# The second layer's places in SBUF: unsplit operands take the longest free, ten w_out units in single tiles, the first input rows asked for ahead of w_in

## The chip, the cores and the metric

One core of one Trainium2 chip runs the whole program. The metric is device time in microseconds (us) of one launch; lower is better. The engines are TensorE (PE, with its weight loads as PEld), VectorE (DVE), ScalarE (ACT), GpSimd (POOL, unused here) and SyncE (SP), which issues nearly all transfers between HBM and SBUF.

## What is computed

Small attention between `x` and a state, in both directions, then two dense layers in float32:

```python
a = softmax(x @ state.T / 8);  xread = a @ state       # per batch and head
a2 = softmax(state @ x.T / 8); sread = a2 @ x
x = concat([xread, sread], axis=2)      # (8, 544, 512) after heads are joined: 4352 rows
h = x @ moe_w_in;  x = (s * relu(h) ** 2 + b) @ moe_w_out       # 512 -> 2048 -> 512
h = x @ moe2_w_in; out = (h / (1 + exp(-h))) @ moe2_w_out       # 512 -> 2048 -> 512
```

## The kernel before

Every product of float32 operands is made of three matmuls: an operand is split into a high part (ACT copies it to fp32r) and a low part (DVE subtracts), and high x high, high x low and low x high are summed in PSUM.

The first layer and the attention run over nine blocks of columns: the eight batches (512 rows each) and a last block `"s"` with the 256 state rows. Each block has 16 steps `f`: `mm1_a(f)` (L634), relu on ACT (L680), square on DVE (L681), `gh` on ACT (L686), `gl` on DVE (L687), and three steps later (`LAG`) `mm2_a(f)` (L701). `r` has three buffers; the block's result is pulled from PSUM into `op` and two `r` buffers, and `end_a` stores it to `x2` in HBM (L739). Block `"s"` runs with the split units of `w_in` themselves: `split_next` splits two units that `load32` (L171, four transfers of 32 rows for each of the two) has brought to a `mid` tile, and asks for the pair two further on.

The second layer is a Strassen-like scheme with seven products `A11 ... A22` instead of eight. Columns are cut into five pieces of 512, 512, 384, 384, 384. **First product** (`first_product`): for each piece, eight `Quad`s of seven steps; a step is one product of six matmuls (L1005), then the operations of `Quad.rest`: pulls of PSUM banks (ACT, L229), sums (DVE, L852), silu (ACT, L1038). `Quad.put` (L1041) writes seven combinations to `go` in HBM. In the middle of a piece `load_inputs` asks for the next piece's eight input tiles (L959), later DVE sums them and ACT and DVE split them. **Second product** (`Chunks`, `Sums`): `go` is read back (L1238), each chunk is split five to six steps ahead, multiplied by the split `w_out`, summed and put out.

All engines run their instructions in the order in which the program issues them; the order is written by hand (`hooks`, `extra`, `after(n, op)`, which runs `op` n steps later).

All of SBUF that the first layer no longer needs is handed to the second one in *places* of 128 x 512 words. `vacate(tag, n)` puts a whole tile of n places into the list `free`. `Place(dtype)` takes one: F32 for unsplit operands (inputs, raw weights, a quad's sums, chunks), F32R for split ones.

```python
of = [k for k, x in enumerate(free) if x[2] is dtype]      # parts of tiles cut for dtype
whole = [k for k, x in enumerate(free) if x[2] is None]    # tiles with all parts free
k = of[0] if of and len(whole) <= 8 else min(of[:1] + whole[:1])
```

A whole tile is cut for one type when its first part is taken; when all its parts have been given back it is whole again (`give`), and the next taker may cut it for the other type. A place is given back in program order, when the last instruction that uses it has been issued; the next taker's first instruction waits until that use has ended.

Of the kernel before, what the change touches and what calls it, by code (L numbers as in the profile page):

```python
# [3 lines left out]

# [1 line left out]

# [6 lines left out]
F32 = mybir.dt.float32  # L13
F32R = mybir.dt.float32r
# [6 lines left out]
B, H, S, NS, D = 8, 8, 512, 32, 64  # L21
DM, DFF = 512, 2048
P = 128
# [10 lines left out]

FIRST_PAIRS = "i0 i1, i2 i3, i4 i5, i6 i7, o0 o1, i8 i9, o2 o3, i10 i11, o4 o5, i12 i13, o6 o7, i14 i15, o8 o9, o10 o11, o12 o13, o14 o15"
PLAIN = (12, 13,)
FIRST = """
L.0.0 L.0.1 L.1.0 L.1.1 Lsbd.0 Lxt.0 A.0.0 Lsg.1 B.0.0.0 B.0.1.0 A.0.1 B.0.2.0 B.0.0.1 B.0.3.0
A.1.0 B.0.1.1 B.1.0.0 B.0.2.1 A.1.1 B.1.1.0 B.1.0.1 B.0.3.1 B.1.1.1 L.2 B.1.2.1 Lsg.2 B.1.2.0
# [25 lines left out]
AGAIN = (8, 9, 10, 11, 6, 7, 4, 5, 0, 1, 2, 3, 8, 9, 10, 11)  # L65
# [8 lines left out]
def fused_kernel(ctx: ExitStack, tc, xt, xn, sbd, sg, w1, w2, sv, bv, out):  # L74
# [29 lines left out]
    def space(tag, shape=(P, S), dtype=F32R):  # L104
        return wpool.tile(list(shape), dtype, tag=tag, name=tag)

    def pair(tag, dtype=F32):
        return space(tag, (P, 2, S), dtype)
# [19 lines left out]
    wh, wl, raw, w32 = {}, {}, {}, {}  # L128
# [16 lines left out]
    def new32(of):  # L145
        if starting and of[0][0] == "i":
            t = flat(rotated("early", "q10 q15 q14" + "".join(f" w{u}" for u in PLAIN)))
        elif starting and of[0][1] in PLAIN:
# [85 lines left out]
    ring = {}  # L234

    def hi_w(w, dve=False):
        t, i = w
        ring[w] = pair(f"w{i}" if t == "o" else f"q{AGAIN[i]}", F32R)
        wh[w] = ring[w][:, 0]
        copy(wh[w], w32[w], dve)  # L240

    def lo_w(w):
        t, i = w
        wl[w] = ring[w][:, 1]
        rest(wl[w], w32[w], wh[w])

    def split(hi, lo, x):
# [90 lines left out]
    two = {}  # L338
# [466 lines left out]
          for k, (_, n) in enumerate(pieces) for p in PRODUCTS}  # L805


    free, closing = deque(), []

    def vacate(tag, n=1):  # L810
        free.append((tag, n, None))

    class Place:
        def __init__(self, dtype=F32R):
            of = [k for k, x in enumerate(free) if x[2] is dtype]
            whole = [k for k, x in enumerate(free) if x[2] is None]
            k = of[0] if of and len(whole) <= 8 else min(of[:1] + whole[:1])
            tag, i, kind, *t = free[k]
            del free[k]
            if not t:  # L820
                two = space(tag, (P, i, S), dtype)
                free.extendleft((tag, n, dtype, two[:, n]) for n in range(i - 1, 0, -1))
                parts[tag], i, t = i, 0, [two[:, 0]]
            self.at, self.t = (tag, i, dtype, t[0]), t[0]

        def give(self):
            tag = self.at[0]
            if closing and tag.startswith("raw"):
                return
            free.append(self.at)  # L830
            whole = [k for k, x in enumerate(free) if x[0] == tag]
            if len(whole) == parts[tag]:
                for k in reversed(whole):
                    del free[k]
                vacate(tag, parts[tag])

    parts = {}

    clock, due = [0], {}

# [596 lines left out]
    def last_block(add):  # L1439

        def give(*tags):
            for tag in tags:
                add(f, 2, vacate, tag)

        splits = [(p, c) for p in RIGHT for c in range(2)]
        inputs[0] = Inputs(0)
        for f in range(NF):
            if f == 0:  # L1450
                give("sbd")
                for tag in ("xt", "xn", "xr0", "xr1", "q12", "q13", "q14"):
                    add(f, 2, vacate, tag, 2)
                for tag in ("xh1", "xl1"):
                    add(f, 2, vacate, tag, 2)
                for i in range(2):
                    add(f, 2, vacate, f"raw{i}", 4)
                add(f, 2, inputs[0].load)
            if f >= 2:
                add(f, 2, vacate, f"w{f - 2}", 2)  # L1460
            if f == 7:
                for tag in ("mid0", "mid1"):
                    add(f, 2, vacate, tag, 2)
                for i in range(4, 8):
                    add(f, 2, vacate, f"q{i}", 2)
            if f == 11:
                for i in range(4):
                    add(f, 2, vacate, f"q{i}", 2)
            if f == 15:
                for i in range(8, 12):  # L1470
                    add(f, 2, vacate, f"q{i}", 2)
            if 2 <= f < 4:
                for name in ("T1", "T2", "T3"):
                    add(f, 2, inputs[0].sum, name, f - 2)
            for i, what in ((f - 4, inputs[0].high), (f - 5, inputs[0].low)):
                if 0 <= i < len(splits) // 2:
                    for p, c in splits[2 * i:2 * i + 2]:
                        add(f, 2, what, p, c)
            for i, what in ((f - 6, "load"), (f - 9, "high"), (f - 10, "low")):
                if i >= 0 and i % 2 == 0 and i // 2 < 5:  # L1480
                    if what == "load":
                        quads[i // 2] = list(duos_in(i // 2))
                    for x in quads[i // 2]:
                        add(f, 2, getattr(x, what))
# [46 lines left out]
    def close():  # L1531

        closing.append(True)
        left = [x for x in free if not x[0].startswith("raw")]
        free.clear()
        free.extend(left)

    def extra(bi):
        k = order[bi]
        ops = {}  # L1540

        def add(f, when, op, *args):
            ops.setdefault((f, when), []).append(lambda: op(*args))

        if bi < B - 1:

            halves = [Half(k + 1, j) for j in range(2)]
            add(1 + (bi == 1), 2, score, k + 1, halves)
            add(1, 2, load_sbd, k + 2)
            add(2, 0, load_all, k + 2, xt)  # L1550
            names = "tr rd nb ex mx sb en n0 n1 n2 s0 s1 s2 s3 s4 tu pl ah al"
            when = (
                (1, 1, 1, 1, 3, 3, 3, 3, 3, 4, 6, 6, 6, 7, 7, 10, 11, 8, 8),
                (2, 2, 2, 2, 5, 5, 5, 5, 5, 8, 9, 9, 9, 10, 10, 10, 11, 11, 12),
            )
            for h, fs in zip(halves, when):
                for n, (f, name) in enumerate(zip(fs, names.split())):
                    add(f + (bi == 1 and n < 4), 2, getattr(h, name))
            add(12, 2, read, k + 1, halves)
            add(13, 0, load_all, k + 2, xn)  # L1560
            add(13, 2, pull_read, k + 1, halves)
        def add_g(f0, fs, *g):
            add(f0, 0, load_g, *g)
            for j in range(2):
                add(fs[j], 2, split_g, *g, j)

        if bi == 1:
            add_g(0, (1, 2), 1, 1)
            for n, u in enumerate(PLAIN):
                add(1 + n, 2, hi_w, ("o", u))  # L1570
                add(1 + n, 2, lo_w, ("o", u))
            one = softmax[1]
            add(0, 0, load_all, 1, xn)
            add(0, 0, load_sbd, 2)
            add(0, 0, load_all, 2, xt)
            for f, when, name, *args in (
                (0, 0, "n0"), (0, 0, "n1"), (0, 0, "n2", 0), (0, 0, "n2", 1), (0, 2, "tu", "a"),
                (0, 2, "pl"), (1, 2, "sr", "a"), (1, 2, "pu"),
            ):
                add(f, when, getattr(one, name), *args)  # L1580
            add(2, 0, load_all, 2, xn)
        if bi < B:

            for fg, (f0, *fs) in enumerate(((1, 4, 4), (3, 6, 7), (9, 12, 13), (11, 14, 15))):
                if fg < 2:
                    g = k, fg + 2
                elif k + 1 < B:
                    g = k + 1, fg - 2
                else:
                    continue  # L1590
                add_g(f0, fs, *g)
        for f in range(NF):
            for when in range(3):
                for op in later.pop((NF * bi + f, when), ()):
                    add(f, when, op)
        if bi == B - 1:
            for i, pair in enumerate(stream[:2]):
                add(5 + 3 * i, 0, load32, pair)
            for i in range(RING // 2):
                add(9 + 2 * i, 2, split_next)  # L1600
        if bi == B:
            for f in (0, 1, 4, 5):
                add(f, 2, split_next)
            last_block(add)
        return ops

    with tc.manual_schedule():
# [8 lines left out]
        act_places.appendleft("q15")  # L1616
        run(order, pend)
        for i in (NF - 2, NF - 1):
            vacate(f"w{i}", 2)
        for n in range(9):  # L1620
            vacate(f"{('r', 'gh', 'gl')[n // 3]}{n % 3}")
        for tag in ("wf0", "wf1", "xs", "q15", "xh0", "xl0", "op"):
            vacate(tag, 2)
        chunks = Chunks()
        to_load = iter([
            Duo(("O", i, p), ("O", i + 1, p)) for p in RIGHT for i in range(0, NF // 2, 2)
# [59 lines left out]
```

## Time and profile before

| | |
|---|---|
| median of 3 runs | 1344.69 us (1343.94 to 1345.14) |
| profiled execution | 1344.56 us, span of its instructions 1342.8 us |
| PE busy | 1303.1 us, 97% of the span |
| DVE, ACT busy | 979.5 us (73%), 705.3 us (53%) |
| mean granted TensorE clock | 0.994 of full speed |
| HBM traffic | 282.95 MB, mean 211 GB/s |

Block `"s"` lies at about 603 to 664 us, the first product follows, the second one ends at 1335, and the last results go out. Pieces 0 and 1 of the first product are at 664 to 739 and 739 to 814, pieces 2 to 4 at 814 to about 1000. Busy times count an instruction from its start to its end; matmuls overlap each other, so a busy PE says that no time without a matmul was seen, not that it is at its peak. A line number like L229 or L852 can be that of a helper (`copy`, `tt`) that many steps share.

### The profile page before, as it was taken

How to read it: one execution, taken by the hardware profiler on the slowest of the kernel's cores; microseconds unless marked ns; L12 is line 12 of the kernel's file. 1: busy time of each engine (PE TensorE's matmuls, PEld its weight loads, DVE VectorE, ACT ScalarE, POOL GpSimd, SP SyncE). 2: the span in 40 equal slices, each digit the busy share in tenths (PEclk: the TensorE clock that was granted, in tenths of full speed). 3: DMA queues.
4: the chain of work that ended last, by engine and by line, in shares of the span. 5: the costliest groups of instructions: out<-in, count | busy, mean ns of one | idle time of the engine just before them, and what ended most of it. 6: DMA issues, size and time to landing. Idle time of an engine off the chain costs nothing. (4 is left out here: it accounts for less than half of the span.)

```text
span 1342.8 us, 20818 instructions
## 1 busy us (share of the span) xinstructions
PE 1303.1 (97%) x7256; PEld 1102.7 (82%) x7256; DVE 979.5 (73%) x1745; ACT 705.3 (53%) x1273; POOL 0.7 (0%) x7
## 2 busy tenths in 40 slices
PE   5999999999999999999999999899999999999997
PEld 1555787888787878888988879899998888899997
DVE  7898798989897979756767647475767766665654
ACT  6885554545454545445655536364666634353542
POOL 0000000000000000000000000000000000000000
PEclk9999999999999999999999999999999999999999
DMA  9975664655555634515576465556699876777583
GB/s 340 323 270 217 224 227 157 205 179 204 189 181 173 206 146 142 195 48 160 156 265 245 184 212 205 199 187 209 219 316 353 286 219 208 209 228 233 167 268 77
DMA packets 171114, 282.95 MB, mean 211 GB/s; under 512 B 22272, under 2 KB 93952, under 8 KB 171008
## 3 DMA queue, kind: packets, MB, share of 16 engines
q1 hardware_dynamic: 170208, 281.22, 62.4%
q8 instruction: 57, 0.93, 0.3%
q10 hardware_dynamic: 800, 0.39, 0.1%
q14 instruction: 49, 0.40, 0.1%
HBM read 166.20 MB, written 115.34 MB: 210 GB/s over the span
## 5 line engine op out<-in xcount | busy, mean ns | idle before, releaser
L701 PE MATMUL bank<-gh,w 128*128 128x512 f32 (+1 forms) x880 | 278.6, 380 | 0.8 <-ACT q L229 0.8
L634 PE MATMUL bank<-xh,q 128*128 128x512 f32 (+1 forms) x624 | 202.8, 374 | 4.4 <-ACT r L680 3.2
L701 PEld LDWEIGHTS bank<-gh,w 128*128 128x128 f32 x880 | 163.8, 189 | 39.1 <-issue 5.9
L701 PE MATMUL bank<-gl,w 128*128 128x512 f32 (+1 forms) x440 | 166.7, 379 | 0.0
L634 PEld LDWEIGHTS bank<-xh,q 128*128 128x128 f32 x624 | 114.4, 189 | 35.9 <-issue 6.9
L681 DVE SCALAR_TENSOR_TENSOR r<-r,s_sb 128x512 f32<-128x512 f32 (+1 forms) x128 | 91.6, 715 | 47.6 <-ACT r L680 47.2
L680 ACT ACTIVATE r<-bank 128x512 f32<-128x512 f32 (+1 forms) x128 | 71.9, 562 | 91.0 <-PE bank L634 74.0
L634 PE MATMUL bank<-xl,q 128*128 128x512 f32 (+1 forms) x312 | 114.9, 368 | 0.0
L686 ACT ACTIVATE gh<-r,b_sb 128x512 fp32r<-128x512 f32 (+1 forms) x96 | 66.5, 693 | 58.5 <-DVE r L681 58.4
L1005 PE MATMUL bank<-q,w 128*128 128x384 f32 (+1 forms) x315 | 92.8, 357 | 3.9 <-DVE q L852 3.9
L701 PEld LDWEIGHTS bank<-gl,w 128*128 128x128 f32 x440 | 83.4, 190 | 15.0
L1005 PE MATMUL bank<-w,w 128*128 128x384 f32 (+1 forms) x319 | 88.0, 355 | 0.0
L701 PE MATMUL bank<-q,w 128*128 128x512 f32 (+1 forms) x384 | 87.5, 377 | 0.0
L1005 PE MATMUL bank<-w,q 128*128 128x384 f32 (+1 forms) x309 | 86.3, 358 | 0.0
L1005 PE MATMUL bank<-q,q 128*128 128x384 f32 (+1 forms) x283 | 81.9, 357 | 3.3 <-ACT q L229 3.3
L687 DVE SCALAR_TENSOR_TENSOR gl<-r,b_sb,gh 128x512 fp32r<-128x512 f32 (+1 forms) x96 | 68.5, 714 | 16.9 <-ACT gh L686 16.8
L701 PEld LDWEIGHTS bank<-q,w 128*128 128x128 f32 x384 | 69.0, 188 | 13.6 <-DVE op L727 0.5
L634 PEld LDWEIGHTS bank<-xl,q 128*128 128x128 f32 x312 | 59.1, 189 | 9.0 <-DVE mid L566 0.2
L1005 PEld LDWEIGHTS bank<-q,w 128*128 128x128 f32 x315 | 58.4, 189 | 9.5 <-DVE q L852 4.9
L229 ACT ACTIVATE q<-bank 128x384 f32<-128x384 f32 (+3 forms) x70 | 42.9, 613 | 39.5 <-PE bank L1005 20.6
L1005 PEld LDWEIGHTS bank<-w,w 128*128 128x128 f32 x319 | 58.6, 188 | 4.9
L1005 PEld LDWEIGHTS bank<-w,q 128*128 128x128 f32 x309 | 56.8, 188 | 5.2
(858 smaller groups left out, 2771.1 us busy)
## 6 DMA issues: line engine op xcount, KB each, us to landing
raw<-w SPq DMA_DIRECT2D x80, 512.0 KB, 5.1
go<-q SPq DMA_DIRECT2D x87, 192.0 KB, 2.0
q<-gd SPq DMA_DIRECT2D x27, 512.0 KB, 5.6
go<-q SPq DMA_DIRECT2D x51, 256.0 KB, 2.4
w<-go SPq DMA_DIRECT2D x68, 192.0 KB, 4.0
w<-go SPq DMA_DIRECT2D x40, 256.0 KB, 4.4
gd<-xr SPq DMA_DIRECT2D x18, 512.0 KB, 4.6
q<-go SPq DMA_DIRECT2D x36, 256.0 KB, 4.8
```

What stands on the lines that cost most here:

```text
L229: nc.scalar.activation(out=out, in_=x, func=AF.Copy)
L634: nc.tensor.matmul(ph[:, :n], a, x, start=j == 0 and i == 0, stop=j == last and i == 2)
L680: nc.scalar.activation(out=r, in_=ph[:, :n], func=AF.Relu)
L681: nc.vector.scalar_tensor_tensor(out=r, in0=r, scalar=s_sb, in1=r, op0=ALU.mult, op1=ALU.mult)
L686: nc.scalar.activation(out=gh, in_=r, func=AF.Identity, bias=b_sb)
L687: nc.vector.scalar_tensor_tensor(out=gl, in0=r, scalar=b_sb, in1=gh.bitcast(F32), op0=ALU.add, op1=ALU.subtract)
L701: nc.tensor.matmul(po[c][:, :n], a, x, start=f == 0 and i == 0, stop=f == NF - 1 and i == 2)
L1005: nc.tensor.matmul(bank[:, :n], a, x, start=start and j == 0 and i == 0, stop=stop and j == last and i == 2, skip_group_check=True,)
```

## The change

Places are now of two kinds. `carve` cuts a tile once, for good, into places of one type (`fixed[F32]` or `fixed[F32R]`). `vacate` hands over tiles of a single place, which either type may take (`spare`). Each place gets a stamp when it is given back. An F32R place comes from `fixed[F32R]` if that isn't empty, otherwise it is the longest free single tile. An F32 place is the longest free of `fixed[F32]` and `spare` together. To have enough single tiles, the split `w_out` units 0 to 9 get two single tiles each, `wh{i}` and `wl{i}`, where each had a pair `w{i}`. In block `"s"`, the operations of `last_block` at f = 0, with the input loads of the second layer's piece 0 (`inputs[0].load`), now stand ahead of that step's `split_next` with its `load32`; at f = 1, 4 and 5 the order is the old one.

```diff
--- before.py
+++ after.py
@@ -1,6 +1,6 @@
 from collections import deque
 from contextlib import ExitStack
-from itertools import islice
+from itertools import count, islice
 
 import numpy as np
 
@@ -34,6 +34,7 @@
 
 FIRST_PAIRS = "i0 i1, i2 i3, i4 i5, i6 i7, o0 o1, i8 i9, o2 o3, i10 i11, o4 o5, i12 i13, o6 o7, i14 i15, o8 o9, o10 o11, o12 o13, o14 o15"
 PLAIN = (12, 13,)
+SINGLE = 10
 FIRST = """
 L.0.0 L.0.1 L.1.0 L.1.1 Lsbd.0 Lxt.0 A.0.0 Lsg.1 B.0.0.0 B.0.1.0 A.0.1 B.0.2.0 B.0.0.1 B.0.3.0
 A.1.0 B.0.1.1 B.1.0.0 B.0.2.1 A.1.1 B.1.1.0 B.1.0.1 B.0.3.1 B.1.1.1 L.2 B.1.2.1 Lsg.2 B.1.2.0
@@ -235,13 +236,16 @@
 
     def hi_w(w, dve=False):
         t, i = w
-        ring[w] = pair(f"w{i}" if t == "o" else f"q{AGAIN[i]}", F32R)
-        wh[w] = ring[w][:, 0]
+        if t == "o" and i < SINGLE:
+            wh[w] = space(f"wh{i}")
+        else:
+            ring[w] = pair(f"w{i}" if t == "o" else f"q{AGAIN[i]}", F32R)
+            wh[w] = ring[w][:, 0]
         copy(wh[w], w32[w], dve)
 
     def lo_w(w):
         t, i = w
-        wl[w] = ring[w][:, 1]
+        wl[w] = ring[w][:, 1] if w in ring else space(f"wl{i}")
         rest(wl[w], w32[w], wh[w])
 
     def split(hi, lo, x):
@@ -805,38 +809,30 @@
           for k, (_, n) in enumerate(pieces) for p in PRODUCTS}
 
 
-    free, closing = deque(), []
-
-    def vacate(tag, n=1):
-        free.append((tag, n, None))
+    spare, closing, stamps = deque(), [], count()
+    fixed = {F32R: deque(), F32: deque()}
+
+    def vacate(*tags):
+        spare.extend((next(stamps), tag) for tag in tags)
+
+    def carve(tag, n, dtype=F32R):
+        t = space(tag, (P, n, S), dtype)
+        fixed[dtype].extend((next(stamps), (tag, i), t[:, i]) for i in range(n))
 
     class Place:
         def __init__(self, dtype=F32R):
-            of = [k for k, x in enumerate(free) if x[2] is dtype]
-            whole = [k for k, x in enumerate(free) if x[2] is None]
-            k = of[0] if of and len(whole) <= 8 else min(of[:1] + whole[:1])
-            tag, i, kind, *t = free[k]
-            del free[k]
-            if not t:
-                two = space(tag, (P, i, S), dtype)
-                free.extendleft((tag, n, dtype, two[:, n]) for n in range(i - 1, 0, -1))
-                parts[tag], i, t = i, 0, [two[:, 0]]
-            self.at, self.t = (tag, i, dtype, t[0]), t[0]
+            self.of = fixed[dtype]
+            if self.of and (dtype == F32R or not spare or self.of[0][0] < spare[0][0]):
+                _, self.tag, self.t = self.of.popleft()
+            else:
+                _, self.tag = spare.popleft()
+                self.t = space(self.tag, dtype=dtype)
 
         def give(self):
-            tag = self.at[0]
-            if closing and tag.startswith("raw"):
-                return
-            free.append(self.at)
-            whole = [k for k, x in enumerate(free) if x[0] == tag]
-            if len(whole) == parts[tag]:
-                for k in reversed(whole):
-                    del free[k]
-                vacate(tag, parts[tag])
-
-    parts = {}
-
-
+            if not isinstance(self.tag, tuple):
+                vacate(self.tag)
+            elif not closing or not self.tag[0].startswith("raw"):
+                self.of.append((next(stamps), self.tag, self.t))
 
     clock, due = [0], {}
 
@@ -1441,34 +1437,36 @@
 
 
         def give(*tags):
-            for tag in tags:
-                add(f, 2, vacate, tag)
+            add(f, 2, vacate, *tags)
 
         splits = [(p, c) for p in RIGHT for c in range(2)]
         inputs[0] = Inputs(0)
         for f in range(NF):
             if f == 0:
                 give("sbd")
-                for tag in ("xt", "xn", "xr0", "xr1", "q12", "q13", "q14"):
-                    add(f, 2, vacate, tag, 2)
-                for tag in ("xh1", "xl1"):
-                    add(f, 2, vacate, tag, 2)
+                for tag in ("xt", "xn", "xr0", "xr1", "q12", "q13"):
+                    add(f, 2, carve, tag, 2, F32)
+                for tag in ("xh1", "xl1", "q14"):
+                    add(f, 2, carve, tag, 2)
                 for i in range(2):
-                    add(f, 2, vacate, f"raw{i}", 4)
+                    add(f, 2, carve, f"raw{i}", 4)
                 add(f, 2, inputs[0].load)
             if f >= 2:
-                add(f, 2, vacate, f"w{f - 2}", 2)
+                if f - 2 < SINGLE:
+                    give(f"wh{f - 2}", f"wl{f - 2}")
+                else:
+                    add(f, 2, carve, f"w{f - 2}", 2)
             if f == 7:
                 for tag in ("mid0", "mid1"):
-                    add(f, 2, vacate, tag, 2)
+                    add(f, 2, carve, tag, 2)
                 for i in range(4, 8):
-                    add(f, 2, vacate, f"q{i}", 2)
+                    add(f, 2, carve, f"q{i}", 2)
             if f == 11:
                 for i in range(4):
-                    add(f, 2, vacate, f"q{i}", 2)
+                    add(f, 2, carve, f"q{i}", 2)
             if f == 15:
                 for i in range(8, 12):
-                    add(f, 2, vacate, f"q{i}", 2)
+                    add(f, 2, carve, f"q{i}", 2)
             if 2 <= f < 4:
                 for name in ("T1", "T2", "T3"):
                     add(f, 2, inputs[0].sum, name, f - 2)
@@ -1531,9 +1529,9 @@
     def close():
 
         closing.append(True)
-        left = [x for x in free if not x[0].startswith("raw")]
-        free.clear()
-        free.extend(left)
+        left = [x for x in fixed[F32R] if not x[1][0].startswith("raw")]
+        fixed[F32R].clear()
+        fixed[F32R].extend(left)
 
     def extra(bi):
         k = order[bi]
@@ -1599,9 +1597,11 @@
             for i in range(RING // 2):
                 add(9 + 2 * i, 2, split_next)
         if bi == B:
-            for f in (0, 1, 4, 5):
+            last_block(add)
+            for f in (0, 1):
                 add(f, 2, split_next)
-            last_block(add)
+            for f in (4, 5):
+                ops[f, 2].insert(0, split_next)
         return ops
 
     with tc.manual_schedule():
@@ -1616,11 +1616,11 @@
         act_places.appendleft("q15")
         run(order, pend)
         for i in (NF - 2, NF - 1):
-            vacate(f"w{i}", 2)
+            carve(f"w{i}", 2)
         for n in range(9):
             vacate(f"{('r', 'gh', 'gl')[n // 3]}{n % 3}")
         for tag in ("wf0", "wf1", "xs", "q15", "xh0", "xl0", "op"):
-            vacate(tag, 2)
+            carve(tag, 2)
         chunks = Chunks()
         to_load = iter([
             Duo(("O", i, p), ("O", i + 1, p)) for p in RIGHT for i in range(0, NF // 2, 2)
```

## Rows read from the trace of the kernel before

**Rows 1.** Busy time by stage: stretch, its length, busy time of each engine, clock, DMA.
```profile
core 0: us, PE busy (x) PEld busy (x) DVE busy (x) ACT busy (x) POOL busy (x), PEclk, DMA share, GB/s
...
600.00:664.00 64.00, 61.37 (x444) 58.63 (x443) 45.16 (x83) 35.48 (x76) 0.00 (x0) 0.97 0.49 152
664.00:739.00 75.00, 75.00 (x332) 61.83 (x331) 52.48 (x84) 45.84 (x81) 0.00 (x0) 1.00 0.72 244
739.00:814.00 75.00, 72.19 (x311) 58.98 (x310) 42.79 (x71) 34.89 (x62) 0.00 (x0) 0.98 0.54 194
814.00:990.00 176.00, 167.56 (x936) 163.44 (x935) 111.62 (x219) 93.55 (x201) 0.00 (x0) 0.99 0.62 214
990.00:1335.00 345.00, 345.00 (x1785) 318.72 (x1784) 218.22 (x407) 167.37 (x336) 0.00 (x0) 1.00 0.74 232
```

**Rows 2.** Waits of PE from 600 to 1000 us: total, times, longest.
```profile
PE bank L1005 <- ACT q L229: 5.5, 3, 3.3
PE bank L1005 <- DVE q L852: 3.9, 3, 2.4
PE bank L634 <- ACT r L680: 2.6, 2, 2.4
PE bank L1005 <- ACT w L229: 1.8, 2, 0.9
```

**Rows 3.** Timeline at three stalls of the first product: start, length, instruction, [idle before].
```profile
780.42 0.84 PE L1005 MATMUL bank<-w,q 128*128 128x512 f32 x3
...
782.59 0.60 ACT L229 ACTIVATE q<-bank 128x512 f32<-128x512 f32 x1 [5.30 <-DMA go<-q]
...
783.25 0.50 PE L1005 MATMUL bank<-xt,q 128*128 128x512 f32 x1 [1.98 <-ACT q L229]
...
855.64 0.49 ACT L229 ACTIVATE q<-bank 128x384 f32<-128x384 f32 x1 [5.70 <-DMA go<-q]
...
951.13 0.44 PE L1005 MATMUL bank<-q,w 128*128 128x384 f32 x1 [0.87 <-DVE q L852]
```

**Rows 4.** Waits of ACT from 664 to 1000 us.
```profile
ACT q L229 <- DMA go<-q: 13.1, 5, 5.7
ACT q L1038 <- DMA go<-q: 12.5, 4, 4.7
```

**Rows 5.** Transfers issued from 660 to 1000 us: number, KB each, median us to landing.
```profile
go<-q SPq DMA_DIRECT2D x82, 192.0 KB, 2.0
go<-q SPq DMA_DIRECT2D x51, 256.0 KB, 2.4
...
q<-x SPq DMA_DIRECT2D x13, 192.0 KB, 4.3
```

**Rows 6.** Busy time and granted clock just after four idle times of PE.
```profile
630.40:633.80 3.40, 3.40 (x19) 3.40 (x18) 2.74 (x6) 3.40 (x8) 0.00 (x0) 0.50 0.02 5
784.00:787.40 3.40, 3.40 (x9) 2.68 (x9) 1.04 (x2) 0.20 (x1) 0.00 (x0) 0.50 0.63 230
855.70:859.10 3.40, 2.92 (x9) 2.92 (x10) 1.03 (x2) 1.22 (x3) 0.00 (x0) 0.50 0.49 174
872.00:875.00 3.00, 1.23 (x7) 1.23 (x8) 2.31 (x5) 1.01 (x2) 0.00 (x0) 1.00 0.07 27
```

**Rows 7.** Busy time while piece 3's inputs are split.
```profile
880.00:890.00 10.00, 10.00 (x60) 10.00 (x59) 9.69 (x21) 8.81 (x21) 0.00 (x0) 1.00 0.49 174
```

**Rows 8.** Timeline at the beginning of block "s".
```profile
609.99 4.37 SPq L171 DMA_DIRECT2D mid<-kept_i  x8
...
616.77 1.38 SPq L959 DMA_DIRECT2D xr<-x  x3
...
618.25 6.75 SPq L171 DMA_DIRECT2D mid<-kept_i  x8
...
621.43 0.69 DVE L852 TENSOR_TENSOR q<-xn,xr 128x512 f32<-128x512 f32 x1 [2.41 <-DMA xn<-x]
...
626.03 0.90 SPq L739 DMA_DIRECT2D x<-r  x2
...
628.75 0.38 ACT L680 ACTIVATE r<-bank 128x256 f32<-128x256 f32 x1 [4.10 <-DMA x<-r]
```

## The prediction, made before the change was run

> **What bounds the kernel now.** I read the views in this order: the busy time by stage, what PE waits for, the timeline at the long waits, the waits of ACT, the times to landing, the granted clock around PE's idle times, and the timeline of block "s". TensorE is the bound: it is busy without a break from 664 to 739 and from 990 to 1335, that is, in piece 0 of the first product and in the whole second product [rows 1]. Between lie the only stretches of the second half that can get shorter: block "s" is 2.6 us short of full, pieces 1 to 4 of the first product 2.8 and 8.4 us [rows 1]. All of this idle time is ended by ACT or DVE, 11.2 us in eight waits in the first product and 2.6 us in two in block "s" [rows 2].
>
> What these two had waited for is in the timeline. The pull of a PSUM bank at 782.59 came 5.30 us late because the place that it writes was still being read by a transfer to `go`; the one at 855.64 came 5.70 us late for the same reason; PE, which needs that bank again two steps later, stood 1.98 us behind the first [rows 3]. ACT alone lost 25.6 us to such transfers in nine waits [rows 4]. The transfer is `Quad.put`: `t4` and `g12` are written out and their places given back at the issue, not at the landing, which is 2.0 to 2.4 us later, and up to 4.3 us after the issue for the input loads that share the queue [rows 5]. The rule in `Place` then hands the same place out at once: with at most 8 whole tiles free it takes the first free F32 half, and there are only a few of those.
>
> Two of the stalls, and the one in block "s", were each followed by 3.4 us at a granted clock of 0.50, the lower level, half of which is lost: 1.7 us each. The one of 2.4 us that ended between 872 and 875 was not [rows 2, 6].
>
> **The change, part by part.** *The order of places.* Takes and gives come in an order that the program fixes, so I stepped both rules through it and counted ages in steps (one step is one product, six matmuls). In pieces 0 to 4, of the places that a quad takes for a sum and that a transfer to `go` had read last, the old rule hands out 38 of 128 within three steps of that transfer and 62 within five; the new one 0 of 145 within three and 7 within five, the youngest four steps old. A step is 1.0 us for 384 columns (60 matmuls in 10 us [rows 7]) and 1.3 us for 512 (six times the 0.22 us between starts in the row of three, 0.84 less 0.39 over two [rows 3]). Four steps of 384 are 4.0 us against about 1 us from the step to its transfer (an estimate: one step, since a put is due one step on) and 2.0 us to land, or 4.3 us if it lands as slowly as an input load. At worst 1.3 us of wait are left, and the bank is needed only two steps later, 2 us. So the stalls that come from these transfers should all go.
>
> What that is worth in the first product: 11.2 us of idle time [rows 2], plus 2 x 1.7 us at half clock [rows 6], plus what idle time leaves out: it starts when the last matmul is modelled to end, 0.39 us after its start, where the next would have started after 0.22 us, so 0.17 us for each of eight waits, 1.4 us; and the first matmul after a wait takes 0.50 instead of 0.39 us [rows 3], 0.1 us each, 0.8 us. Together 16.8 us. Of that I leave 0.9 us: the stall that ended at 951.13 stood 0.87 us on DVE [rows 3] in a stretch where the splits of the next piece's inputs are under way, and in the like stretch of the piece before DVE was busy 9.69 of 10 us and ACT 8.81 [rows 7]; engines that full will not keep up everywhere. Sum: 15.9 us gained. Bounds: nothing, if the waits return elsewhere; 16.8 us, if all go.
>
> *Input rows ahead of w_in.* In block "s", step f = 0, eight loads of 256 KB move ahead of one `load32` (eight small transfers) on SP. Now SP issues `load32` for 4.37 us from 609.99, the inputs from then (614.4) to 618.15, the second `load32` of f = 1 for 6.75 us, because it can't run further ahead of the landing inputs, and only then the stores of block 7's result, `x<-r` at 626.03; the relu at 628.75 waits 4.10 us for that store, since it writes the same `r` [rows 8]. PE's longest wait there, 2.4 us, is for that relu [rows 2]. After the change the same 24 issues stand ahead of the store: the inputs 3.8 us, a `load32` held back by their landing 6.75 us, one not held back 3.8 to 4.4 us. That is 14.3 to 14.9 us against 14.9, so the store goes out 0 to 0.6 us earlier; I take 0.5. The sum at 621.43, for which DVE stood 2.41 us [rows 8], finds its rows 4.4 us sooner and costs nothing; this removes PE's small wait of 0.2 us (2.6 less 2.4 [rows 2]). So 0.7 us of idle time goes, 1.9 us stays. Whether so short a stop still lowers the clock is open from the rows (1.98 us did, 2.4 us did not [rows 2, 3, 6]), so I count half of 1.7 us. Gain 1.5 us; bounds 0 (the order alone frees nothing) and 4.6 us (2.6, 1.7 and 2 x 0.17 us). The `load32` that is moved back lands by about 622 and is split at f = 4, at 629 or a little before: covered; if it weren't, ACT and DVE would stand in a block where PE has no reserve.
>
> *w_out units in single tiles, and F32R halves that stay F32R.* No instruction is added, and no byte moved. An F32R place is taken from the pinned halves first, so in the second product 468 of its 577 takes get a place that the step just issued has given back. The split of the chunk five to six steps ahead then can't start before PE ends that step. ACT needs 0.6 us [rows 3] and DVE 0.7 us [rows 8] for 512 columns, 1.3 us against five steps of 1.3 us. Hidden by that lead, at nothing. From below it could gain nothing, since PE has no idle time there [rows 1]; from above see the third rival.
>
> Sum: 15.9 + 1.5 = 17.4 us from the profiled execution's 1344.56 us (its span is 1342.8; the 1.8 us around it stay), which is 0.13 us below the median of the runs: **1327.2 us**.
>
> **The rivals.** *Part of the stalls stays (0.15).* For: DVE and ACT are nearly full while a piece's inputs are split [rows 7], and with PE no longer stopping they get 17 us less. If half of the 16.8 us stays and block "s" gives nothing, 1344.6 - 8.4 = 1336 us.
>
> *The waits only move (0.06).* The places are as many as before; if they are simply too few, any order hands out young ones. Then each stall finds another taker, and the time is 1342 to 1346. Against it: ages of four steps and more, counted above, and 4 to 20 places free for an F32 take in pieces 1 to 4, counted in the same way. The Trainium skill, page "Perfetto Trace Analysis", section "Optimization Strategy", says that the same gap repeating on the engine that should be full can mean that there isn't enough SBUF for the next tile. By that rule more places would be needed, an order would not do, and the sum would be 0. The trace speaks for a shortage of old places, not of places.
>
> *Slower: splits tied to PE's steps in the second product (0.05).* The place of a split is one that PE is still reading. It decides if the splits' lead of five steps is used up where a product ends and DVE has up to four more operations of 0.7 us, at 35 ends (five pieces, seven products). If PE then stood one step, 1.0 us, at each: 35 us lost, 17 gained, 1344.6 + 35 - 17 = 1363 us; it turns to slower at 0.5 us an end. Against: DVE is busy 218 of 345 us there, ACT 167 [rows 1], and a lead of 5 us stands against 2.8 us of extra work.
>
> **How the numbers follow.** My forecast has 0.74, with a range of its own of 1322 to 1332: 16.8 and 4.6 us gained make 1323, less 1 us because these idle times rest on modelled ends, and three quarters of the 16.8 us with nothing from block "s" make 1332. To hold eight in ten, the range for all cases takes in the nearer half of the first rival, up to 1335. A measurement of this kernel tells about 0.2% from no change, 2.7 us. Faster by more: the forecast and the first rival, 0.89. Within: 0.06. Slower: 0.05.
>
> **What the next profile would show.** Right: ACT's waits on `go<-` transfers fall from 25.6 us to a few, PE is full in pieces 1 to 4 but for about 1 us, and the first product has no stretch at clock 0.50. In block "s" the inputs are issued at 610 and DVE no longer waits for them, while one wait of the relu on `x<-r` of some 3.5 us is left with a PE idle time near 1.9 us. The second product stays full, with more and shorter waits of ACT and DVE for PE. Wrong: PE idle times in pieces 1 to 4 that end on a DVE or ACT without a transfer behind it (first rival), waits on `go<-` as long as now (second), or PE waiting for splits after 1000 us (third).

## The result and the profile after

The changed kernel takes 1326.12 us (median of four, 1325.49 to 1327.87) against 1344.91 us for the kernel before in the same runs: ratio 0.986, 95% interval 0.9843 to 0.9877, some 18.8 us faster. The profiled execution took 1325.49 us, its span is 1323.6 us, the mean granted clock 0.997. One execution of a later run, the places alone, took 2177 us at a mean granted clock of 0.56 and is left out there. Line numbers move: the product of the second layer is L1001 now, the relu L684, `gl` L691, the pull or high part L230, the sum L848, the input loads L955.

First the busy time by stage, as in [rows 1]; the stages end a little earlier, so their bounds are moved.

```profile
core 0: us, PE busy (x) PEld busy (x) DVE busy (x) ACT busy (x) POOL busy (x), PEclk, DMA share, GB/s
600.00:664.00 64.00, 61.54 (x451) 58.50 (x450) 46.43 (x86) 36.74 (x80) 0.00 (x0) 1.00 0.50 154
664.00:739.00 75.00, 75.00 (x332) 62.10 (x332) 53.68 (x85) 45.93 (x81) 0.00 (x0) 1.00 0.71 244
739.00:812.00 73.00, 73.00 (x324) 60.45 (x323) 45.33 (x75) 37.56 (x68) 0.00 (x0) 1.00 0.60 219
812.00:985.00 173.00, 173.00 (x995) 172.50 (x995) 119.15 (x232) 101.20 (x214) 0.00 (x0) 1.00 0.69 236
985.00:1315.00 330.00, 330.00 (x1698) 303.72 (x1698) 225.00 (x388) 173.86 (x316) 0.00 (x0) 1.00 0.70 228
```

Pieces 1 to 4 are full, where 11.2 us had been missing [rows 1, 2], and none of these stretches has a granted clock under 1.00 [rows 6]. What PE still waits for from 600 us to the end (total, times, longest) is two waits, both in block `"s"`:

```profile
PE bank L638 <- ACT r L684: 1.5, 1, 1.5
PE bank L705 <- DVE gl L691: 0.9, 1, 0.9
```

The two largest groups of ACT's waits on transfers to `go` were 25.6 us [rows 4]; with the smaller groups it was 36.7 us for ACT and 9.6 us for DVE. These are all that are left from 660 to 990 us, of ACT and of DVE:

```profile
ACT xr L230 <- DMA go<-q: 0.9, 1, 0.9
...
ACT xn L230 <- DMA go<-xt: 0.6, 1, 0.6
```

```profile
DVE wh L848 <- DMA go<-r: 1.3, 1, 1.3
...
DVE wl L848 <- DMA go<-wl: 0.5, 1, 0.5
```

Where did the 19.2 us of span go (1342.8 less 1323.6)? I measure block `"s"` from the start of its first matmul to that of the first product's first, and each of the two products from the start of its first matmul to that of its own last. The first product went from 344.68 to 327.24 us, 17.44 less. Block `"s"` went from 58.91 to 57.27, 1.64 less. The second product took 326.65 both times, and block `"s"` began at 604.99 and 604.94. These stage lengths are what I compare below: the work ahead of block `"s"` varies by some microseconds from one execution to the next (the first product of the same kernel began at 662.2 us once and at 666.1 another time), so totals can't tell effects of 1 us apart, while the second product is 326.65 us in every run that leaves it alone.

The beginning and end of block `"s"` in the timeline, which answers to [rows 8]:

```profile
609.89 0.42 SPq L955 DMA_DIRECT2D sbd<-x  x1
...
612.26 2.25 SPq L955 DMA_DIRECT2D xr<-x  x3
614.60 9.11 SPq L172 DMA_DIRECT2D mid<-kept_i  x16
...
624.75 0.89 SPq L743 DMA_DIRECT2D x<-r  x2
...
627.38 0.38 ACT L684 ACTIVATE r<-bank 128x256 f32<-128x256 f32 x1 [5.14 <-DMA x<-r]
...
654.02 0.63 ACT L230 ACTIVATE w<-q 128x512 fp32r<-128x512 f32 x1 [1.98 <-PE bank L705]
...
658.21 0.68 DVE L233 TENSOR_TENSOR wl<-q,wh 128x512 fp32r<-128x512 f32 x1
658.81 0.48 DVE L691 SCALAR_TENSOR_TENSOR gl<-r,b_sb,gh 128x256 fp32r<-128x256 f32 x1
...
659.34 0.39 PE L705 MATMUL bank<-gl,w 128*128 128x256 f32 x1 [0.92 <-DVE gl L691]
```

The inputs are asked for at 609.9 and no sum waits for them any more. The store `x<-r` goes out at 624.75 instead of 626.03, and the relu still waits for it, the first of PE's two waits. The second wait is new. At 654.02 ACT writes a high part into a `w` pair that PE still reads. By the order of the program this is `w11`: both kernels give it back at `f = 13`, while `mm2`, three steps behind, reads that unit last at `f = 14`, but only the new rule, by which a split takes a place cut for F32R first, hands it out in that same step. ACT stands 1.98 us for PE, the splits reach DVE in a heap (four from 656.40 to 658.89), and `gl` comes late behind them.

### The profile page after: what moved, and what is told of

Read it like the earlier page. It is cut to its first block, busy times and chain, and to the rows that moved or that the text cites. A ratio compares the mean times of both kernels' runs of the same rounds, so it can differ in the third digit from the quotient of the medians.

```text
span 1323.6 us, 21087 instructions
## 1 busy us (share of the span) xinstructions
PE 1295.6 (98%) x7256; PEld 1099.2 (83%) x7256; DVE 998.6 (75%) x1745; ACT 723.9 (55%) x1273; POOL 0.7 (0%) x7
## 4 chain that ended last, share of the span: by engine, by line
PE 90%; DMA 3%; DVE 3%; ACT 1%; SPq 1%; issue 1%; DVEq 0%; ACTq 0%
PE bank L1001 49%; PE bank L705 25%; PE bank L638 13%; DMA raw<-w 2%; PE bank L290 1%; PE bank L353 1%; PE bank L717 1%; PE bank L366 1%; DMA xt<-xt 1%; SPq L172 0%; PE bank L460 0%; ACT q L186 0%; SPq L955 0%; DVE q L233 0%; DMA mid<-kept_i 0%
## 5 line engine op out<-in xcount | busy, mean ns | idle before, releaser
L1001 PE MATMUL bank<-q,q 128*128 128x384 f32 (+1 forms) x446 | 125.7, 354 | 0.0
L684 ACT ACTIVATE r<-bank 128x512 f32<-128x512 f32 (+1 forms) x128 | 71.9, 562 | 87.9 <-PE bank L638 72.5
L705 PE MATMUL bank<-gh,w 128*128 128x512 f32 (+1 forms) x352 | 110.5, 378 | 0.0
L705 PE MATMUL bank<-gh,wh 128*128 128x512 f32 (+1 forms) x264 | 100.7, 382 | 0.3 <-ACT q L230 0.3
L705 PE MATMUL bank<-gh,wl 128*128 128x512 f32 (+1 forms) x264 | 99.9, 378 | 0.0
L705 PE MATMUL bank<-gl,wh 128*128 128x512 f32 (+1 forms) x264 | 99.8, 378 | 0.0
L1001 PEld LDWEIGHTS bank<-q,q 128*128 128x128 f32 x446 | 81.9, 188 | 6.5
L691 DVE SCALAR_TENSOR_TENSOR gl<-r,b_sb,gh 128x512 fp32r<-128x512 f32 (+1 forms) x96 | 68.4, 713 | 17.8 <-ACT gh L690 17.7
L705 PEld LDWEIGHTS bank<-gh,w 128*128 128x128 f32 x352 | 65.0, 188 | 13.9 <-issue 1.7
L705 PE MATMUL bank<-gl,w 128*128 128x512 f32 (+1 forms) x176 | 66.5, 378 | 0.9 <-DVE gl L691 0.9
L1001 PE MATMUL bank<-q,w 128*128 128x384 f32 (+1 forms) x213 | 60.8, 354 | 0.0
L705 PEld LDWEIGHTS bank<-gh,wl 128*128 128x128 f32 x264 | 49.7, 188 | 9.3
L705 PEld LDWEIGHTS bank<-gl,wh 128*128 128x128 f32 x264 | 49.7, 188 | 9.0
L705 PE MATMUL bank<-q,wh 128*128 128x512 f32 (+1 forms) x192 | 56.4, 377 | 0.0
L1001 PE MATMUL bank<-w,q 128*128 128x384 f32 (+1 forms) x152 | 49.2, 356 | 0.0
```

What stands on the lines that cost most here:

```text
L684: nc.scalar.activation(out=r, in_=ph[:, :n], func=AF.Relu)
L691: nc.vector.scalar_tensor_tensor(out=gl, in0=r, scalar=b_sb, in1=gh.bitcast(F32), op0=ALU.add, op1=ALU.subtract)
L705: nc.tensor.matmul(po[c][:, :n], a, x, start=f == 0 and i == 0, stop=f == NF - 1 and i == 2)
L1001: nc.tensor.matmul(bank[:, :n], a, x, start=start and j == 0 and i == 0, stop=stop and j == last and i == 2, skip_group_check=True,)
```

## The experiments

Ratios are to the kernel before on the same chip; "stage" is the first product's length as above.

**The order alone** (before, with the four `split_next` and `last_block` in the new order).

```diff
         if bi == B:
-            for f in (0, 1, 4, 5):
-                add(f, 2, split_next)
             last_block(add)
+            for f in (0, 1):
+                add(f, 2, split_next)
+            for f in (4, 5):
+                ops[f, 2].insert(0, split_next)
```

> The old rule of places, with only the input loads moved ahead of the step's load32 in block s. If the two parts add up, the first product keeps its stalls (344.7 us from its first to its last matmul) and block s gains what the changed kernel gained there: the clock drop of 1.7 us gone, PE idle 1.5 instead of 2.6 us, some 2.8 us, so about 1342 us. If the order does nothing by itself and block s gained through the places, 1344.9 us.

Measured: 1344.28 us, ratio 0.9976 (0.9962 to 0.999). Block `"s"` 56.26 us, 2.65 less than before; the stage 346.51, with all its stalls. That is 1.8 us more than before: one stop, at 789, took 2.6 us instead of 0.8. PE's waits after 600 us, and the clock after the stop in block `"s"`, which was 0.83 in the same ten microseconds of before:

```profile
PE bank L1005 <- ACT q L229: 5.8, 3, 3.4
PE bank L1005 <- DVE q L852: 3.9, 3, 2.5
PE bank L1005 <- ACT w L229: 3.5, 2, 2.6
PE bank L634 <- ACT r L680: 1.7, 1, 1.7
```

```profile
630.00:640.00 10.00, 10.00 (x86) 10.00 (x85) 9.34 (x19) 9.56 (x22) 0.00 (x0) 1.00 0.32 80
```

**The places alone** (the changed kernel with the old order, the same diff the other way round).

> The new rule of places and the single tiles, with the old order in block s. If the ages of places are what stalled the first product, it runs through in 327 us as in the changed kernel, and block s has its old stall of 2.4 us with the clock drop behind it: about 1328.5 to 1329.5 us. If the earlier inputs were needed for the first product too, its stalls come back in part and the time is above 1333 us.

Measured: 1326.68 us (five runs, 1326.02 to 1331.71), ratio 0.9855 (0.9831 to 0.988), below the 1328.5 to 1329.5 us expected. The stage is 327.24 us, all of the gain; block `"s"` takes 59.31, with no gain (0.4 us more than before). The 2 us by which this block is longer than in the changed kernel do not show in the total, which varies by more than that.

```profile
PE bank L638 <- ACT r L684: 2.2, 1, 2.2
PE bank L705 <- DVE gl L691: 0.9, 1, 0.9
```

```profile
630.00:640.00 10.00, 8.63 (x60) 8.64 (x61) 7.96 (x16) 8.80 (x20) 0.00 (x0) 0.83 0.79 258
```

**The new kinds of places, handed out young** (the changed kernel; an F32 place comes from the places cut for F32 whenever there is one, not from the longest free).

```diff
-            if self.of and (dtype == F32R or not spare or self.of[0][0] < spare[0][0]):
+            if self.of:
```

Stepped through in the same way as for the prediction, this rule hands out 66 of 168 such places within three steps of the transfer that read them.

> The changed kernel, pinned halves and single tiles as they are, but an F32 take prefers the F32 halves to the single tiles, as F32R does. Counted in steps, 66 of 168 places that a transfer to go read last are then handed out within three steps of it (0 of 145 with the longest free; 38 of 128 before). If age is the cause, the stalls come back at least as large as before: first product 340 us or more, 1340 to 1355 us. If it is the tiles (halves that aren't made whole and cut again, a tile of one place that waits for nobody's other half), it stays at 1326 to 1329 us.

Measured: 1378.26 us, ratio 1.0223 (1.0199 to 1.0248), slower than before, and by more than the 1340 to 1355 us expected. The stage is 376.71 us, and even piece 0, full in both kernels, has lost 7.2 us. PE's waits (the four largest), ACT's on `go`, and piece 0:

```profile
PE bank L1001 <- ACT xr L230: 8.0, 2, 4.9
PE bank L1001 <- ACT q L230: 7.2, 2, 6.4
PE bank L1001 <- ACT xn L230: 7.1, 3, 4.4
PE bank L1001 <- ACT r L230: 5.7, 1, 5.7
```

```profile
ACT xr L1034 <- DMA go<-xr: 22.6, 5, 7.9
...
ACT xn L230 <- DMA go<-xn: 16.7, 4, 6.8
ACT q L1034 <- DMA go<-q: 11.7, 3, 4.8
```

```profile
664.00:739.00 75.00, 67.82 (x293) 55.54 (x292) 42.75 (x68) 37.50 (x66) 0.00 (x0) 0.95 0.63 207
```

**The old rule, with places given back three steps later** (before; nothing else is touched).

```diff
-                self.give(name)
+                after(3, self.give, name)
...
-                after(1, self.give, "g21", "t2")
+                after(4, self.give, "g21", "t2")
```

> The kernel before, but a place that a quad's last transfer reads is given back three steps later than the issue; tiles, rule and order are the old ones. If age is the cause, most of the 18 us of the first product goes with this alone: 1326 to 1334 us. If it is the kind of tiles, nothing changes: 1344 us.

Measured: 1332.16 us, ratio 0.9887 (0.9865 to 0.9908). The stage is 330.29 us: 14.4 of the 17.4 us, in the old tiles, under the old rule. Block `"s"` stays at 58.85. Stepped through once more, this kernel still hands out 31 places within three steps of the transfer's issue (38 before), but none within one step; the kernel before hands out nine, all in the very step of the issue, and all of them places that the sum `g12` had held. So "within three steps" is too wide a mark, by this count: the takes in the first step are the ones that go together with the stalls.

```profile
PE bank L634 <- ACT r L680: 2.5, 1, 2.5
PE bank L1005 <- ACT w L229: 1.8, 1, 1.8
PE bank L1005 <- ACT q L229: 0.7, 1, 0.7
```

**The changed kernel once more**, beside the next three on one chip.

> The changed kernel once more, as the measure for the next ones on the same chip: first product 327.2 us without a stall, 1325 to 1328 us.

Measured: 1327.91 us, ratio 0.9863 (0.9842 to 0.9884); stage 327.24, block `"s"` 57.43.

**Both types take the longest free.**

```diff
-            if self.of and (dtype == F32R or not spare or self.of[0][0] < spare[0][0]):
+            if self.of and (not spare or self.of[0][0] < spare[0][0]):
```

> The changed kernel, but F32R takes the longest free of both lists too, so that a split's place in the second product was given back six steps ago or more, not in the step just issued. Counted in steps, 29 of 150 places that a transfer to go read last go to a quad within five steps of it (7 of 145 in the changed kernel), 5 of them within three. If the splits tied to PE's steps cost something, the second product gets shorter than 326.65 us; I expect it the same to 0.1 us. If young F32 places stall PE, the first product is longer than 327.2 us by the stall of a few of these, 1 to 5 us.

Measured: 1325.94 us, ratio 0.9849 (0.983 to 0.9869); stage 327.67, less of a loss than the 1 to 5 us expected; second product 326.65, the same, as expected. That F32R keeps to the places cut for it, and leaves the older single tiles to the unsplit operands, is worth 0.4 us of the stage. In block `"s"` the new wait is gone (55.98 us).

**No single tiles** (`SINGLE = 0`: all w_out units stay pairs).

> The changed kernel with no w_out unit in single tiles (all sixteen in pairs, pinned to F32R). Counted in steps, 22 of 161 places that a transfer to go read last go to a quad within five steps, 2 of them within one, none else within three. If the single tiles matter by the ages that they give, little is lost: up to 3 us in the first product, 1326 to 1330 us. If they matter by themselves, as tiles of which no half holds up the other, the stalls come back: over 1335 us.

Measured: 1326.33 us, ratio 0.9856 (0.9835 to 0.9877); stage 327.91, 0.7 us longer than with ten; block `"s"` 56.15, again without the new wait.

**Block "s" without its store wait** (the changed kernel; the `load32` of `f = 1` goes out at `f = 2`, behind the stores, and at `f = 15` the weights `q8` to `q11` are handed over ahead of the w_out unit).

```diff
...
-            for f in (0, 1):
-                add(f, 2, split_next)
+            add(0, 2, split_next)
+            add(1, 2, lambda: split_next(load=False))
+            add(2, 2, load32, stream[-1])
```

> The changed kernel with the two waits that are left in block s taken away: the load32 of f = 1 is asked for at f = 2, behind the stores of block 7's result, and the tiles q8 to q11 are handed over ahead of w13 at f = 15, so that the splits of that step don't wait for the matmuls that still read w12 and w13. If these two are what PE's waits of 1.5 and 0.9 us come from, block s falls from 57.3 to about 54.5 us and the time by 2.5 us, to 1323.5 us. If the relu waits for the store anyway, or the w_in units come late, the gain is below 1 us.

Measured: 1325.6 us, ratio 0.9846 (0.9825 to 0.9867); block `"s"` 55.49 us, 1.8 less, where 2.8 had been expected of the two waits. The wait of the relu is gone; the one for `gl`, 0.9 us, is as before, so its cause was not at `f = 15`.

**Shorter lead of the splits in the second product.** The changed kernel splits six high parts and five low parts of the chunks ahead of it. With three and two:

```diff
-        for n in range(6):
+        for n in range(3):
             add(last, 45 + 2 * n, chunks.high)
-        for n in range(5):
+        for n in range(2):
             add(last, 47 + 2 * n, chunks.low)
```

> The changed kernel with the splits of the second product three and two steps ahead of their matmuls, not six and five. It asks for the point from which the third rival decides. If the lead is what hides that a split can't start before PE ends the step, PE now stands in the second product, which was 326.65 us: where products end, at up to 35 places, up to 1 us each, 5 to 35 us in all. If the splits fit into one step even there, nothing is lost.

Measured, a single run: 1326.38 us against 1349.57 for before beside it; second product 326.68 us, PE without a wait in it, and none of the 5 to 35 us expected.

With two and one:

> As e9_short_split_lead, with the splits two and one steps ahead. A low part's subtraction can then start only when PE ends the step before the one that needs it, 0.5 to 0.7 us and a semaphore. By the tie of splits to PE's steps PE stands 0.5 to 1 us in each of 280 steps: 140 to 280 us more. If the tie were loose (old places after all), it stays near 327 us.

Measured, a single run: 1517.35 us; second product 518.23 us, 191.6 longer. Its first 52 of 280 steps still take about 1.36 us each, as with the long lead. Then, behind the end of a product, DVE has two more sums (L848) and two transposes (L1167) to do, and shortly after the last of these PE waits for the first time (DVE and PE):

```profile
1058.26 0.68 DVE L848 TENSOR_TENSOR wl<-bank,wl 128x512 f32<-128x512 f32 x1
1058.86 0.68 DVE L233 TENSOR_TENSOR xl<-sbd,op 128x512 fp32r<-128x512 f32 x1
1059.46 0.70 DVE L1167 STREAM_TRANSPOSE raw<-wl 128x512 f32<-128x512 f32 x1
...
1062.06 0.50 PE L1001 MATMUL bank<-op,xl 128*128 128x512 f32 x1 [0.61 <-DVE op L233]
```

It waits in every step from there on but the last. A later stretch of the timeline (PE, ACT and DVE) shows the cycle:

```profile
1100.60 1.43 PE L1001 MATMUL bank<-q,w 128*128 128x512 f32 x5 [0.61 <-DVE q L233]
1101.83 0.63 ACT L230 ACTIVATE q<-wl 128x512 fp32r<-128x512 f32 x1 [1.64 <-PE bank L1001]
1101.86 0.39 PE L1001 MATMUL bank<-xl,w 128*128 128x512 f32 x1
1102.12 0.69 DVE L233 TENSOR_TENSOR q<-gh,xl 128x512 fp32r<-128x512 f32 x1 [1.57 <-PE bank L1001]
1102.86 0.50 PE L1001 MATMUL bank<-q,w 128*128 128x512 f32 x1 [0.61 <-DVE q L233]
```

PE ends a step; only then may ACT (0.63 us) and DVE (0.69 us) write the places that it read; PE starts on what they wrote. A step takes 2.26 us (from 1100.60 to 1102.86) instead of the 1.36 us of a full PE.

**The best version: each pair of w_out places one step later**, on top of the mended block `"s"`.

```diff
-            if f >= 2:
-                if f - 2 < SINGLE:
-                    give(f"wh{f - 2}", f"wl{f - 2}")
-                else:
-                    add(f, 2, carve, f"w{f - 2}", 2)
+            if 2 <= f < SINGLE + 2:
+                give(f"wh{f - 2}", f"wl{f - 2}")
+            if f >= SINGLE + 3:
+                add(f, 2, carve, f"w{f - 3}", 2)
...
-        for i in (NF - 2, NF - 1):
+        for i in (NF - 3, NF - 2, NF - 1):
```

> As e8_block_s_mended, and the pairs w10 to w13 are handed over one step later, when the matmuls that read them last have been issued (in the changed kernel w11 is handed over at f = 13 and read by PE at f = 14, and ACT stood 1.98 us for that at 654). If that is where the wait of 0.9 us near 659 comes from, block s falls by another 1.1 us, from 55.5 to 54.4 us, and the first product stays at 327.2 us: 1 us below e8. If not, 55.5 us again.

Measured: 1323.5 us (five runs, 1322.61 to 1324.58), ratio 0.984 (0.9827 to 0.9854). Block `"s"` takes 54.29 us and is full; PE has no wait at all from 600 us to the end.

```profile
600.00:664.00 64.00, 64.00 (x464) 60.87 (x463) 48.22 (x88) 39.37 (x83) 0.00 (x0) 1.00 0.54 161
```

## Why the prediction was right, step by step

The time was predicted as 1327.2 us, within 1322 to 1335, and measured as 1326.12; the likeliest case is the one that came.

**The stalls of the first product come from places that a transfer to `go` still reads.** Right, and shown from three sides. The places alone take all stalls away. The same kinds of places handed out young bring more of them than before, 66 takes within three steps against 38, with ACT waiting on `go` again. The prediction's 25.6 us for ACT's waits on `go` is the sum of the two groups in [rows 4] alone; all of them were 36.7 us, which makes its case stronger, not weaker. And the old tiles under the old rule lose most of their stalls when a place only comes back three steps later. So what counts is the time from the transfer's issue to the next take, and by the count of steps the first step after it above all: nine takes there before, none in the changed kernel and with places given back later, two without the single tiles, where the stage lost only 0.7 us. Single tiles and the split into kinds matter as a way to it (0.7 us without the tiles, 0.4 us without the preference).

**15.9 us in the first product.** Measured 17.44. The term that was mis-sized is the 0.9 us left for the stall that ended at 951.13, on the ground that DVE and ACT are nearly full there [rows 3, 7]. It did not stay: pieces 2 to 4 are full. The sum of idle time, clock and restarts, 16.8 us, was itself 0.6 short. Of this, 0.2 us lies in piece 0 (76.41 us before, 76.19 after, from its first matmul to piece 1's first), which the sum left out because neither profile shows a wait there; for the rest the runs don't tell which part was short.

**1.5 us in block "s".** Measured 1.64, but out of other parts. The store goes out 1.28 us earlier (predicted 0.5, bounds 0 to 0.6): the inputs took 4.6 us of SP and the next sixteen issues of `load32` 9.11 us together, where I had put one `load32` that is held back at 6.75 us and one that isn't at 3.8 to 4.4. The wait behind it is 1.5 us, not 1.9. The drop of the clock, counted half, is wholly gone; the order alone shows the two together, 2.65 us. Against that stands 1.0 us that I had not foreseen: the wait for `gl` at 659, which the places alone have too and the order alone has not. Its cause is that the new rule of places hands out `w11` a step before PE's last reader of it is issued: the best version, in which the pairs come one step later, is without it, and so are the two kernels that take the places of that moment in another order (both types the longest free, no single tiles).

**The second product costs nothing.** Right: 326.65 us in both, with no wait of PE.

**First rival, part of the stalls stays.** It did not; engines that are nearly full kept up.

**Second rival, the waits only move.** It fell: the total of ACT's and DVE's waits on `go` is 3.3 us, where it was 46.3, and no other wait of PE took their place in the first product. The Trainium skill, page "Perfetto Trace Analysis", section "Optimization Strategy", which had been weighed beside it, gives too little SBUF as a possible cause of the same gap repeating. By it these stalls would have wanted more places; measured, the same number of places was enough, taken in another order.

**Third rival, splits tied to PE.** The tie exists. It is hidden by the lead, as forecast, and a lead of three high and two low parts still hides it. But the price I gave to it, 1 us at each of 35 ends of products, was the wrong shape. At a lead of two and one it does begin where the prediction said, at an end of a product where DVE has four more operations, but PE does not catch up behind it: it is paid at nearly every step from there on, 191.6 us in all. Between these two leads it goes from nothing to all.

**What stays open.** Whether the clock falls after a stop: see below.

## What to carry to other kernels

A place in SBUF is free when its last reader has ended, and a transfer out of it is a reader that ends some microseconds after its issue (2.0 to 2.4 us here [rows 5]): where an engine at the bound waits for others that wait for such transfers, hand out the places that have been free the longest before looking for more of them. The same age has to be kept at a handover between two stages, where the last reader may not even be issued yet: one w_out unit handed over one step early gave back 1.0 of 2.65 us. Where operands are split just ahead of use into places that PE is reading, know the lead at which the engines fall into step, since with a shorter one nearly every step pays.

## What was not expected of the hardware

A stop of PE of about 2 us is followed by a granted clock of 0.50 at some times and not at others. In the kernel before, stops of 1.98 and 2.42 us were followed by 3.4 us at 0.50 and one of 2.36 us was not [rows 6]. With the order alone, stops of 2.09 us at 782, almost that of 1.98 us before, and of 2.6 us at 789 were not; with the places handed out young, stops of 2.1 and 2.3 us were. In block `"s"`, stops of 1.0 to 1.8 us never were in any run, those of 2.2 to 2.5 us were. No run here tells what decides.

SP issues more slowly when transfers ahead are slow to land: sixteen issues of `load32` took 9.11 us in the changed kernel, of which the last nine took 4.02, and eight took 6.75 before [rows 8]. The trace says what SP stands for. In the kernel before, these are its two largest waits from 618 to 626 us, while it issues the eight:

```profile
SPq L171 <- DMA xn<-x: 1.9, 2, 1.5
SPq L171 <- DMA xr<-x: 1.7, 3, 1.1
```

Each issue that waited so began within 0.02 us of the landing of the transfer eight issues ahead of it, whose semaphore it waits for: the program uses eight of them in turn for its transfers, so it is this limit that shows here, and no run tells whether the queue itself has one. So a store behind a burst of loads is late by the burst's landing, not only by its number of issues.
